# Earlier inputs, other PSUM banks and half products: three edits around the first steady unit of a fused recurrence and maxout FFN

## The chip, the cores and the metric

The kernel runs on one NeuronCore of a Trainium2 chip. The metric is the device time of one execution in microseconds; the number for a kernel is the median over its runs. Everything is FP32 on the device.

## The reference

A gated linear recurrence (an attention block) is computed for 4 batches x 8 heads over 768 tokens with head size 48; its output, with the heads side by side, is the input of a maxout FFN.

```python
# q, k, v, f_logit: (4, 8, 768, 48)
f = 1.0 / (1.0 + np.exp(-f_logit))
for t in range(S):
    state = f[:, :, t, :, None] * state + np.einsum('bhd,bhe->bhde', k[:, :, t], v[:, :, t])
    y[:, :, t] = np.einsum('bhd,bhde->bhe', q[:, :, t], state)
x = y.transpose(0, 2, 1, 3).reshape(3072, 384)
h = np.maximum(np.maximum(x @ w1, x @ w2), x @ w3)      # w1, w2, w3: (384, 768)
return h @ w_out                                        # w_out: (768, 384)
```

## The kernel before

The sequence is cut into chunks of 64 tokens. A **unit** is one chunk of two batches, 128 token rows, with all 8 heads; there are 24 units (`NU`). Four units make a **group** of 512 tokens (`TOK`), and the FFN is run by groups, six of them.

For one unit u these helpers emit the work:

- `load` and `load_v` issue DMAs on the sync queue (SP). For u below 8 (`BY_ROWS`), f, k and q come as one DMA each with token rows on the partitions, v as two DMAs. f, k and q have four slots by u mod 4, and v has four tiles (`NLD`), so unit 4 writes where unit 0 was read.
- `sigmoids` turns f into gates: for u below 8, TensorE transposes the rows into PSUM (`transposed`, L278) and ScalarE applies the sigmoid (L295).
- `scan`, `after`, `before`: VectorE's running products of the gates (L316, L334), and k and q multiplied by them (kh at L327, qh at L338). k and q reach these through `features`, which for u below 8 are TensorE transposes as well.
- `keys` (L354), `pairs` (L379, masked by VectorE at L382), `values` (L394 or L398), `sums` (L419, added to the state by VectorE at L427) and `finish` (L465) or, for the first four units, `y_by_tokens` (L438, L443) and `x_of_tokens` (L454) compute the unit's output and carry the state. `pack` moves a finished group into the layout of the FFN by DMA.

PSUM has several small pools with their own banks: `ps_tr` (two tiles named "tr") for transposes, `ps_f` (two tiles named "p") for FFN products, `ps_a` and `ps_y` with one tile each. For units 0 to 3, k and q are turned in the "p" banks, for units 4 to 7 in "tr"; f always in "tr".

`ffn` is a generator. For each of six column blocks j of the hidden layer it emits three **products**, one for each of w1, w2, w3: three matmuls of 128 x 512 accumulate into one "p" bank (L513), and then ScalarE copies the first product out (L518) or VectorE takes the maximum (L520). For group 0 the first two blocks are done in two halves of 256 tokens, which makes 12 small products ahead of 12 of full width. Then come four **output products**, each six matmuls of 128 x 384 (L538), a copy and two DMAs. `fill(n)` resumes the generator until it has yielded n times. A small product has one yield, a full or an output product has two, both behind it; so `fill(2)` is one full product, and of two `fill(1)` in a row one does a product and the other nothing.

The weights arrive as 64-bit words in 24 **pieces** (18 of w1 to w3, 6 of w_out), 12 of them in raw buffers at a time, and are rounded to FP32 on the device: ScalarE (L228, L229, L232), VectorE (L239, L240, or L242 from the tenth piece on) and GpSimd (L246). Nine pieces are issued before the first unit's work; the others by `load_weights(2, done)` (L208), called in `ffn` after each product of group 0, which also emits the next rounding.

The order on every engine is the order of the code (`manual_schedule`): a prologue written out by hand for units 0 to 3 and the loads of unit 4, then a loop over units 4 to 23. The prologue's end and the loop's fills are:

```python
                y_by_tokens(3)
                load(GRP, one, "q")
...
                fill(2)
                before(GRP)
                carry(GRP)
                fill(2)
                for u in range(GRP, NU):
                    n = u + 1
                    fill(0 if u == 2 * GRP else 4 if u % 2 and u > 2 * GRP else 2)
...
                    fill(1 if u < 2 * GRP else 2)
```

Of the kernel before, what the change touches and what calls it, by code (L numbers as in the profile page):

```python
# [55 lines left out]
def kernel(  # L56
# [20 lines left out]
    NJ = DFF // 128  # L77
    GRP = 4
    TOK = GRP * UT
# [9 lines left out]
    def fast():  # L89
        ctx = ExitStack()  # L90
        with ctx:
# [74 lines left out]
            def load(u, queues=one, names="fkq"):  # L166
                for nm, src in (("f", f_logit), ("k", k), ("q", q)):
                    if nm not in names:
                        continue
                    if u < BY_ROWS:  # L170

                        c, bp = divmod(u, 2)
                        queues[NAMES.index(nm) % 2].dma_start(  # L173
                            out=rows[nm][u % 4][:, :, 0:D],
                            in_=src[2 * bp:2 * bp + 2, :, c * C:(c + 1) * C, :].rearrange("b h t d -> t b h d"))
                    elif u % 2 == 0:
                        t0 = u // 2 * C
                        for n in range(C // 32):
                            for par in range(2):
                                for e0, w in ((0, 32), (32, D - 32)):  # L180
                                    p0 = par * DP + e0
                                    nc.sync.dma_start(
                                        out=blocks[nm][u // 2 % 2][p0:p0 + 32, n, :, 0:w],
                                        in_=src[:, par::2, t0 + n * 32:t0 + (n + 1) * 32, e0:e0 + w].rearrange(
                                            "b h t d -> t (b h) d"))

            def load_v(u, queues=one):
                load_tokens(v_tiles[u % NLD], v, u, queues)
# [85 lines left out]
            def transposed(nm, u, name="tr"):  # L274

                t = {"tr": ps_tr, "p": ps_f}[name].tile([128, HP, 2, C], FP32, name=name)
                for hp in range(HP):
                    nc.tensor.transpose(t[:, hp].rearrange("p a t -> p t a"), slots[nm][u % 4][:, hp * 128:(hp + 1) * 128],  # L278
                                        ident)
                return t.rearrange("p h a t -> p a h t")  # L280
# [20 lines left out]
            def features(nm, u):  # L301

                if u < BY_ROWS:
                    return transposed(nm, u, "p" if u < GRP else "tr")
                t = work.tile([128, 2 * HP, C], FP32, name=f"{nm}t", bufs=1)
                turned(t, block(nm, u))
                return by_batch(t)
# [3 lines left out]
            def scan(u):  # L311
                gate = gate_tiles[u % 2]
                if u >= BY_ROWS:
                    turned(gate[:, :, 1:], ready[u])
                r = r_tiles[u % 2]
                nc.vector.tensor_tensor_scan(r[:, 0:LEN][:, ::-1], flat(gate)[:, ::-1], flat(from_one)[:, ::-1], 1.0,  # L316
                                             op0=ALU.mult, op1=ALU.max)
                whole = r[:, 0:LEN].rearrange("p (x t) -> p x t", t=C + 1)[:, :, 1]
                nc.vector.reciprocal(from_inv[u % 2][:, :, 0], whole)
# [85 lines left out]
            def sums(u):  # L405

                d, v_ld = ready[u], v_tiles[u % NLD]
                y = d["y"]
                if u < NU - 2:


                    apart = u < GRP
                    if apart:
                        y = ps_a.tile([128, 2, 512], FP32, name="a")
                    Y = HP * C
                    for hp in range(HP):
                        for par, a in FOUR:
                            s = slice(a * C, (a + 1) * C)
                            nc.tensor.matmul(y[par * DP:(par + 1) * DP, a, Y + hp * D:Y + (hp + 1) * D],  # L419
                                             lhsT=d["ks"][s, 2 * hp + par, :], rhs=v_ld[s, 2 * hp + par, 0:D],  # L420
                                             start=apart and hp == 0, stop=(hp == HP - 1), skip_group_check=True)
                    ds = y[:, :, Y:Y + HP * D]
                    new = states[u % 2].rearrange("p (a h) d -> p a (h d)", a=2)
                    if u < 2:
                        nc.scalar.copy(new, ds)  # L425
                    else:
                        nc.vector.tensor_tensor(new, ds, d["state"].rearrange("p (a h) d -> p a (h d)", a=2), op=ALU.add)  # L427
# [66 lines left out]
            def ffn(g, xT):  # L494
                hm = work.tile([128, NJ, TOK], FP32, name="hm", bufs=1)


                steps = [(j, slice(0, TOK)) for j in range(NJ)]
                if g == 0:
                    steps = [(j, slice(n * HALF, (n + 1) * HALF)) for n in range(2) for j in range(J_HALF)] + steps[J_HALF:]  # L500
                done, n_step = 1, 0
                for j, t in steps:
                    w = t.stop - t.start
                    for i in range(3):
                        p = ps_f.tile([128, TOK], FP32, name="p")[:, 0:w]
                        for kt in range(NK):
                            if g:
                                rhs = xT[:, kt, :]
                            elif w < TOK:
                                rhs = by_halves(xT)[:, t.start // HALF, kt, :]  # L510
                            else:
                                rhs = by_halves(xT)[:, :, kt, :]
                            nc.tensor.matmul(p if g or w < TOK else p.rearrange("p (two t) -> p two t", two=2),  # L513
                                             lhsT=w_in[i][:, kt, j * 128:(j + 1) * 128], rhs=rhs,
                                             start=(kt == 0), stop=(kt == NK - 1))
                        if i == 0:
                            top = work.tile([128, TOK], FP32, name="top")[:, 0:w]
                            nc.scalar.copy(top, p)  # L518
                        else:
                            nc.vector.tensor_tensor(hm[:, j, t] if i == 2 else top, p, top, op=ALU.max)  # L520

                        if g == 0:
                            n_step += 1
                            ahead = n_step + 1 if n_step <= 6 else 7 + (n_step - 6) * 5 // 6 if n_step <= 12 else 12 + (n_step - 12) * 6 // 5
                            for r in range(done, min(ahead, len(pieces))):
                                if r + 2 < len(pieces):
                                    round_begin(r + 2)
                                if r + 1 < len(pieces):
                                    round_end(r + 1)
                                done = r + 1  # L530
                            load_weights(2, done)
                        yield
                        if w == TOK:
                            yield
                for i in range(GRP):
                    p = ps_f.tile([128, TOK], FP32, name="p")
                    for j in range(NJ):
                        nc.tensor.matmul(p[:, 0:DM], lhsT=hm[:, j, i * UT:(i + 1) * UT], rhs=w_out[:, j, :],  # L538
                                         start=(j == 0), stop=(j == NJ - 1))
                    o = work.tile([UT, DM], FP32, name="o", bufs=3)  # L540
                    nc.scalar.copy(o, p[:, 0:DM])  # L541
                    c, bp = divmod(g * GRP + i, 2)
                    for a in range(2):
                        t0 = (2 * bp + a) * S + c * C
                        last = g * GRP + i == NU - 1 and a
                        (nc.scalar if last else nc.sync).dma_start(out=out[t0:t0 + C, :], in_=o[a * C:(a + 1) * C, :])
                    yield
                    yield

            pending = []  # L550
# [24 lines left out]
            with tc.manual_schedule():  # L575
# [25 lines left out]
                y_by_tokens(0)  # L601
                keys(1)
                sums(0)
                scan(2)
                after(2)
                pairs(1)
# [23 lines left out]
                fill(1)  # L630
                keys(3)
                sums(2)
                load(GRP, one, "fk")
                y_by_tokens(2)
                pairs(3)
                fill(1)
# [4 lines left out]
                sums(3)  # L641
                fill(1)
                y_by_tokens(3)
                load(GRP, one, "q")
                load_v(GRP)
                load(GRP + 1)
                load_v(GRP + 1)
                x_of_tokens(3, xT)
# [324 lines left out]
```

## Time and profile before

| | us |
|---|---|
| median of 10 runs | 480.62 (478.46 to 482.48) |
| the profiled execution | 479.17 |
| its span (first to last instruction) | 477.4 |
| TensorE busy in the span | 457.6 (96%) |
| VectorE, ScalarE, GpSimd busy | 267.0, 145.8, 104.3 |
| mean granted TensorE clock | 0.994 |

A row of a timeline or a group tells the engine, the line, the tiles written and read, the shape and the count. TensorE shows two records for each FP32 matmul. "SPq" is the sync engine's queue issuing a DMA: its duration is the time of the issue, not of the transfer. A wait is put down to what released it last. A chain of waits follows the end of the program back to its beginning.

### The profile page before, as it was taken

What the parts mean: (1) busy time and instruction counts of PE and PEld (TensorE: products, weight loads), DVE (VectorE), ACT (ScalarE), POOL (GpSimd) and SP (SyncE); (2) the same over time, 40 slices, a digit from 0 to 9 for tenths busy, and PEclk for the clock granted to TensorE, in tenths of its full rate; (3) what the DMA queues carried; (4) which work ended last, traced back from release to release, by engine and by line L of the source; (5) the groups of instructions that cost most, each with busy time, mean ns of one, the idle gap of its engine ahead of it and who ended that gap; (6) DMA issues with size and microseconds to landing.
All of it is one profiled execution on the core that took longest, in us unless ns stands there. A gap on an engine that the chain in (4) does not pass through costs nothing.

```text
span 477.4 us, 10233 instructions
## 1 busy us (share of the span) xinstructions
PE 457.6 (96%) x4068; PEld 250.4 (52%) x4068; DVE 267.0 (56%) x528; ACT 145.8 (31%) x339; POOL 104.3 (22%) x125
## 2 busy tenths in 40 slices
PE   4989699999999999999999999999999999999995
PEld 3877555555555445554455554455554445544453
DVE  6876476767487584577684587694575220021110
ACT  2444367522012133243243243243343211100000
POOL 2153444432330230320330321330311300000000
PEclk9999899999999999999999999999999999999999
DMA  9999996215477444576634487534470012100002
GB/s 134 217 286 266 211 206 82 45 35 94 84 97 113 115 82 104 96 144 88 153 68 109 92 150 89 160 69 106 95 146 4 0 51 50 35 1 1 2 17 52
DMA packets 177141, 47.13 MB, mean 99 GB/s; under 512 B 154816, under 2 KB 175552, under 8 KB 177088
## 3 DMA queue, kind: packets, MB, share of 16 engines
q1 hardware_dynamic: 172528, 45.25, 48.4%
q10 hardware_dynamic: 4560, 1.18, 1.5%
q8 instruction: 33, 0.54, 0.5%
q14 instruction: 20, 0.16, 0.1%
HBM read 37.75 MB, written 4.72 MB: 89 GB/s over the span
## 4 chain that ended last, share of the span: by engine, by line
PE 88%; SPq 3%; DMA 3%; DVE 3%; ACTq 1%; issue 1%; ACT 0%; DVEq 0%
PE p L513 59%; PE p L538 18%; PE y L465 3%; PE y L398 2%; SPq L173 2%; PE a L379 2%; PE y L419 2%; DMA q_ld<-in_q_dram 2%; DMA raw<-in_moe_w_dram 1%; PE tr L278 1%; SPq L163 1%; ACTq L486 1%; DVE r L316 1%; DVE prod L334 0%; PE tr L354 0%
## 5 line engine op out<-in xcount | busy, mean ns | idle before, releaser
L513 PE MATMUL p<-xT,w_in 128*128 128x512 f32 (+1 forms) x684 | 291.1, 577 | 0.4 <-POOL w_in L246 0.4
L513 PEld LDWEIGHTS p<-xT,w_in 128*128 128x128 f32 x684 | 127.5, 191 | 133.2 <-issue 125.6
L538 PE MATMUL p<-w_out,hm 128*128 128x384 f32 x288 | 96.3, 489 | 0.0
L520 DVE TENSOR_TENSOR top<-p,top 128x512 f32<-128x512 f32 (+1 forms) x38 | 24.9, 656 | 104.8 <-PE p L513 104.8
L538 PEld LDWEIGHTS p<-w_out,hm 128*128 128x128 f32 x288 | 54.0, 190 | 37.6 <-issue 1.9
L369 DVE STREAM_TRANSPOSE ks<-kh 32x128 f32<-32x128 f32 x224 | 67.7, 302 | 3.6
L518 ACT COPY top<-p 128x512 f32<-128x512 f32 (+1 forms) x38 | 21.4, 562 | 150.6 <-PE p L513 150.6
L326 POOL COPY ends<-r 128x8 f32<-128x8 f32 x24 | 6.7, 277 | 188.0 <-DVE r L316 188.0
L520 DVE TENSOR_TENSOR hm<-p,top 128x512 f32<-128x512 f32 (+1 forms) x38 | 24.8, 652 | 34.4 <-PE p L513 34.4
L327 POOL TENSOR_TENSOR kh<-kt,r 128x512 f32<-128x512 f32 x16 | 31.4, 1961 | 36.5 <-DVE kt L283 23.9
L541 ACT COPY o<-p 128x384 f32<-128x384 f32 x24 | 11.4, 476 | 86.7 <-PE p L538 83.3
L316 DVE TENSOR_TENSOR_SCAN r<-gate,from_one 128x520 f32<-128x520 f32 x24 | 29.8, 1240 | 10.9 <-ACT gate L295 7.0
L471 ACT COPY heads<-y 64x256 f32<-64x256 f32 (+1 forms) x60 | 22.2, 369 | 44.9 <-PE y L465 38.5
L334 DVE TENSOR_TENSOR_SCAN prod<-gate,from_inv 128x520 f32<-128x520 f32 x24 | 30.8, 1285 | 0.0
L246 POOL TENSOR_TENSOR w_in<-top_bits,rest_bits 128x384 uint32<-128x384 uint32 x18 | 20.3, 1133 | 35.6 <-DVE top_bits L242 15.8
L382 DVE TENSOR_TENSOR at<-a,mask 128x512 f32<-128x512 f32 x24 | 16.5, 689 | 12.0 <-PE a L379 11.6
L283 DVE STREAM_TRANSPOSE gate<-sig 128x512 f32<-128x512 f32 x16 | 11.3, 705 | 15.5 <-ACT sig L298 15.5
L344 POOL TENSOR_TENSOR state<-st,ends 128x384 f32<-128x384 f32 x22 | 19.2, 873 | 0.7 <-ACT st L425 0.6
L338 POOL TENSOR_TENSOR qh<-qt,prod 128x512 f32<-128x512 f32 x16 | 18.9, 1179 | 0.6 <-DVE qt L283 0.5
L398 PEld LDWEIGHTS y<-at,v_ld 64*64 64x64 f32 x640 | 11.1, 134 | 14.1 <-issue 9.0
L465 PEld LDWEIGHTS y<-qh,state 48*48 48x48 f32 x640 | 10.3, 119 | 12.7 <-issue 11.6
L379 PE MATMUL a<-qh,kh 48*64 48x64 f32 x768 | 16.2, 223 | 0.2
(89 smaller groups left out, 311.9 us busy)
## 6 DMA issues: line engine op xcount, KB each, us to landing
raw<-in_moe_w_dram SPq DMA_DIRECT2D x36, 384.0 KB, 6.0
v_ld<-in_v_dram SPq DMA_DIRECT2D x48, 96.0 KB, 3.6
raw<-in_moe_w_out_dram SPq DMA_DIRECT2D x12, 384.0 KB, 4.5
out_dram<-o SPq DMA_DIRECT2D x47, 96.0 KB, 2.2
xT<-heads SPq DMA_DIRECT2D x30, 72.0 KB, 2.2
f_ld<-in_f_logit_dram SPq DMA_DIRECT2D x32, 64.0 KB, 2.6
k_ld<-in_k_dram SPq DMA_DIRECT2D x32, 64.0 KB, 2.6
q_ld<-in_q_dram SPq DMA_DIRECT2D x32, 64.0 KB, 3.1
```

The lines of the kernel that those rows point to most:

```text
L316: nc.vector.tensor_tensor_scan(r[:, 0:LEN][:, ::-1], flat(gate)[:, ::-1], flat(from_one)[:, ::-1], 1.0, op0=ALU.mult, op1=ALU.max)
L327: (nc.vector if u < BY_ROWS else nc.gpsimd).tensor_tensor(kh.rearrange("p h a t -> p a h t"), kt, by_batch(r[:, 1:LEN + 1].rearrange("p (x ...
L334: nc.vector.tensor_tensor_scan(flat(prod), flat(gate_tiles[u % 2]), flat(from_inv[u % 2]), 1.0, op0=ALU.mult, op1=ALU.max)
L369: nc.vector.transpose(ks[n * 32:(n + 1) * 32, :, par, e0:e0 + 32], kh[p0:p0 + 32, :, a, t0:t0 + 32])
L379: nc.tensor.matmul(p[t, par, hp * C:(hp + 1) * C], lhsT=kh[r, hp, a, :], rhs=qh[r, a, hp, :], start=True, stop=True)
L398: nc.tensor.matmul(y[o:o + DP, a, hp * C:(hp + 1) * C], lhsT=v_ld[s, 2 * hp + par, :], rhs=d["at"][s, par, hp, :], start=(hp == 0), stop=F ...
L465: nc.tensor.matmul(y[o:o + D, a, hp * C:(hp + 1) * C], lhsT=st[r, a, hp, :], rhs=d["qh"][r, a, hp, :], start=False, stop=(hp == HP - 1), s ...
L471: nc.scalar.copy(heads[o, :, t0 + a * C:t0 + (a + 1) * C], y[i, a, 0:HP * C].rearrange("p (h t) -> p h t", h=HP))
L513: nc.tensor.matmul(p if g or w < TOK else p.rearrange("p (two t) -> p two t", two=2), lhsT=w_in[i][:, kt, j * 128:(j + 1) * 128], rhs=rhs, ...
L518: nc.scalar.copy(top, p)
L520: nc.vector.tensor_tensor(hm[:, j, t] if i == 2 else top, p, top, op=ALU.max)
L538: nc.tensor.matmul(p[:, 0:DM], lhsT=hm[:, j, i * UT:(i + 1) * UT], rhs=w_out[:, j, :], start=(j == 0), stop=(j == NJ - 1))
```

## The change

Three edits. The loads of unit 4 (f, k, q and v) are issued after `sums(0)` in the code; on the sync queue this is right behind the nine early weight pieces and ahead of the tenth. `features` turns k and q of unit 3 in the "tr" banks in place of the "p" banks. In `ffn` a full product yields after its second matmul of three and at its end, and an output product after its third matmul of six and at its end, where both yields stood at the end before. The number of yields is the same.

```diff
@@ features
-                    return transposed(nm, u, "p" if u < GRP else "tr")
+                    return transposed(nm, u, "p" if u < GRP - 1 else "tr")
@@ ffn
                             nc.tensor.matmul(p if g or w < TOK else p.rearrange("p (two t) -> p two t", two=2),
                                              lhsT=w_in[i][:, kt, j * 128:(j + 1) * 128], rhs=rhs,
                                              start=(kt == 0), stop=(kt == NK - 1))
+                            if kt == 1 and w == TOK:
+                                yield
...
                         yield
-                        if w == TOK:
-                            yield
                 for i in range(GRP):
                     p = ps_f.tile([128, TOK], FP32, name="p")
                     for j in range(NJ):
                         nc.tensor.matmul(p[:, 0:DM], lhsT=hm[:, j, i * UT:(i + 1) * UT], rhs=w_out[:, j, :],
                                          start=(j == 0), stop=(j == NJ - 1))
+                        if j == NJ // 2 - 1:
+                            yield
...
-                    yield
                     yield
@@ prologue
                 keys(1)
                 sums(0)
+                load(GRP)
+                load_v(GRP)
                 scan(2)
...
                 sums(2)
-                load(GRP, one, "fk")
                 y_by_tokens(2)
...
                 y_by_tokens(3)
-                load(GRP, one, "q")
-                load_v(GRP)
                 load(GRP + 1)
                 load_v(GRP + 1)
```

## The prediction

> **What bounds the kernel now.** I read the page first (engine totals, the 40 slices), then TensorE's waits, then timelines and windows around the longest of them.
>
> ```profile
> PE 457.6 (96%) x4068; PEld 250.4 (52%) x4068; DVE 267.0 (56%) x528; ACT 145.8 (31%) x339; POOL 104.3 (22%) x125
> ...
> PE   4989699999999999999999999999999999999995
> ...
> PEclk9999899999999999999999999999999999999999
> DMA  9999996215477444576634487534470012100002
> ```
>
> TensorE is busy everywhere but in slices 1, 3 and 5 (slice 5 is 47.7 to 59.7 us, and the clock dips there too). After about 60 us a gain can only come from work that TensorE no longer waits for. The DMA engines are full in the first six slices, so there each load's place in the order counts. TensorE's waits:
>
> ```profile
> PE tr L278 <- DMA q_ld<-in_q_dram: 4.2, 1, 4.2
> ...
> PE p L438 <- DVE st L427: 0.9, 1, 0.9
> PE y L465 <- DVE st L427: 0.8, 1, 0.8
> ...
> PE p L278 <- ACT top L518: 0.5, 1, 0.5
> ```
>
> The first, third and fourth stand where the diff works. The timeline of TensorE around the first (start, duration, instruction), and two windows (window, length, busy time and count of PE, PEld, DVE, ACT, POOL; then clock, DMA share, GB/s):
>
> ```profile
> 44.76 2.76 PE L513 MATMUL p<-xT,w_in 128*128 128x256 f32 x12
> 51.72 0.90 PE L278 MATMUL tr<-ident,q_ld 128*128 128x128 f32 x4 [4.20 <-DMA q_ld<-in_q_dram]
> 52.41 6.80 PE L513 MATMUL p<-xT,w_in 128*128 128x256 f32 x24
> ```
>
> ```profile
> 48.00:51.70 3.70, 0.00 (x0) 0.02 (x1) 2.02 (x4) 1.47 (x4) 2.58 (x2) 1.00 1.23 198
> 51.70:55.40 3.70, 3.69 (x12) 3.06 (x13) 0.88 (x2) 0.00 (x0) 0.00 (x0) 0.54 1.10 152
> ```
>
> A product of the first group at half width is 6 records. TensorE ends products 7 and 8, stands until q of unit 4 lands, and then runs at clock 0.54 for 3.7 us. The sync queue shows why q is late: it is issued at 42.99, behind six weight pieces, and takes 8.6 us to land.
>
> ```profile
> 23.61 8.52 SPq L208 DMA_DIRECT2D raw<-in_moe_w_dram  x10
> 32.22 0.95 SPq L173 DMA_DIRECT2D f_ld<-in_f_logit_dram  x1
> 33.26 3.95 SPq L173 DMA_DIRECT2D k_ld<-in_k_dram  x1
> 37.31 4.96 SPq L208 DMA_DIRECT2D raw<-in_moe_w_dram  x5
> 42.38 0.52 SPq L208 DMA_DIRECT2D raw<-in_moe_w_out_dram  x1
> 42.99 0.68 SPq L173 DMA_DIRECT2D q_ld<-in_q_dram  x1
> ```
>
> **Part 1, the loads of unit 4.** Five issues move: f and k from 32.2 and 33.3, q from 43.0, the two of v from 43.8 and 46.5, all to about 27.8, right after the ninth piece (the tenth is issued there now). What they overwrite was last read by unit 0, whose last reader, the sums at L419 (TensorE, start 22.55), is done by 23.2; so I add no wait on the sync queue. Nothing of this goes through POOL's or ACT's queue.
> How long do they take in the DMA engines? By landing times, q of unit 5 is down 1.5 us after its k (56.7 and 55.2), k and q of unit 6 are 1.2 and 1.3 us after the load before: 1.3 us for each of f, k, q, and about as much for the two halves of v, 5.2 us in all. The window 50 to 56 us says the same: 4708 packets in 6.0 us, nearly all under 512 B, and the four loads are 4 x 1024 packets of 192 B.
> A rule speaks against the move. The Trainium skill, "DMA: Bandwidth & Descriptors", Specifications, asks for at least 512 B per transfer for line rate; putting small packets in front of the 1 KB packets of the weights then costs dearly. If each 192 B packet cost as much as 512 B at the 341 GB/s which that page's table gives for 1 MB, 4096 of them take 6.1 us (an estimate from the page). I take the trace's 5.2; the sum below is the same with either, because what pays is the next item.
> Who is later: piece 10 lands at 27.84 + 8.9 = 36.8 now, and at about 42.0 then (42.9 by the rule). Its first user is the ACT rounding at L228, start 46.52; cover 4.5 us. Pieces 11 to 14 follow at some 1.1 us each (42 to 47), against roundings at 48.0 and then, after product 10, from about 50.9. So they cost nothing. Were that cover gone, ACT is in order: behind the rounding stand the copy of product 10's bank, the keys of unit 4 and the sigmoid of unit 5, and TensorE would stand microsecond for microsecond. From f of unit 5 on, the same bytes lie ahead as before, so those loads land when they do now.
> What goes: the 4.20 us wait, since q lands near 40. And the slow clock: q's transposes and 24 records took 52.41 - 51.72 + 59.04 - 52.41 = 7.32 us; at full clock a record of this kind starts every 0.216 us (12 in 2.59) and the four transposes take 0.44, so 5.6; 1.7 us goes with the wait.
> What comes instead: vector work that ran in the shadow of the wait. DVE does the scan of before(4) (48.82, 1.23 us), then qh at L338 (0.69), and only then empties product 9's bank (L520, 0.42): 51.2 us. TensorE, with two banks, reaches product 11 at 47.5 + 0.44 + 2.59 = 50.5. New wait +0.7, between 0 (if the scheduler's wait is looser than I read) and 1.0.
> What is late next: f of unit 5. Its landing is not in the trace; between the second half of v (46.52 + 6.7 = 53.2) and k of unit 5 (49.88 + 5.3 = 55.2) I put it at 54.2. Its transposes start at 60.20 now and at 60.20 - 4.20 - 1.7 + 0.7 = 55.0 then: 0.8 us of cover, the thinnest of all. k and q of unit 5 have about 3 us (63.27 and 63.71 less 5.2, against 55.2 and 56.7), f of unit 6 nearly 5 (74.74 - 5.2 against 59.35 + 5.3). Part 1: -4.2 - 1.7 + 0.7 = -5.2 us.
>
> **Part 2, k and q of unit 3 in the transpose banks.** Same 8 transposes. The 0.5 us wait of q's transposes on ACT L518 at 27.5 should go, for the transpose banks' last readers there (24.17 + 0.46 at the latest) are done. But TensorE waits again at 32.72 for DVE L427, and DVE's rows from 22.58 to 32.68 are back to back: qh (30.18) waits for DVE's own scan of 1.86 us. The time moves from one wait to the other: 0 us, bounds -0.1 and +0.3 (later users of these banks, keys of unit 3 at 30.64 and x at 35.33, find kh and qh finished at 26.9 and 30.9). If DVE were not the chain here, it would be worth 0.5.
>
> **Part 3, halves.** No instruction is added; only odd fills differ, in units 4 to 7. In units 4 and 6 the last fill leaves the third matmul of a product to the next unit, and with it the bank's emptying and the rounding emitted there (one piece on ACT, DVE and POOL); all weight issues are past by then, so SP is untouched. In unit 7 the last fill, empty now, gets the second half of an output product, 6 records of 0.32 us = 1.94 us, between the sums at L419 (end 109.0) and finish(7) at L465; its copy and two output DMAs follow it, behind the loads of unit 10 on SP, and nothing waits for them.
>
> ```profile
> 108.39 0.63 PE L419 MATMUL y<-v_ld,ks 64*64 64x48 f32 x32
> 109.80 0.66 PE L465 MATMUL y<-qh,state 48*48 48x64 f32 x32 [0.78 <-DVE st L427]
> ```
>
> The wait lasts until DVE's 0.56 us are over (109.19 + 0.56), so 1.94 covers it: -0.8 us, from then on to the end, as TensorE has only one wait of 0.3 us later. Against it: held-open banks could stall a product; at most one copy, 0.4 us, in units 5 and 7. I take -0.8, bounds -0.8 and 0.
>
> **Sum.** -5.2 + 0 - 0.8 = -6.0 us. The profiled execution took 479.17 (span 477.4 and 1.77 around it); it becomes 473.2. It lies 1.45 below the median of the ten runs, 480.62, which becomes **474.6**.
>
> **Rivals.**
> A, f of unit 5 becomes the wait. For it: 0.8 us of cover at an estimated landing, and the sync queue stalls for 2 to 4 us in single rows. Against: DMA is full around it, so order alone moves nothing. Two us late leaves -4.0: 476.6. Here the clock matters again. The trace has one gap long enough to show a loss, 4.2 us for 1.7, pro rata 0.8 for 2 us. The skill ("TensorE: Matmul & The Clock Gate", Part 1: The HAM clock gate) says only an idle window of about 3.4 us, free-running, halves the clock; then 2 us costs none. The 0.9 us wait at 32.72 ran on at clock 1.00, so I follow the rule; by the row it is 477.4.
> B, slower: the sync queue blocks at the moved issues. Its rows for such loads show up to 2.04 us for f, 3.95 for k, 2.40 for q, and 2.67 and 1.22 for the halves of v: 12.3 us if all five fall out so at 27.8, in place of 5.2, with everything behind 7.1 later. f of unit 5 lands at 61.3, 6.3 after TensorE asks; with the clock's 1.7 the sum is -6.0 + 8.0 = +2.0: 482.6. It decides from a landing after about 59.3. Against it: those stalls end as earlier loads land (k's at 37.2, when piece 10 is down at 36.8), so they are the engines' own backlog, already in 5.2.
> C, the move is no move: q's issue is held for something late (a bank or tile read that I missed) and only part 3 acts: -0.8, 479.8, no change that can be told.
>
> **How the numbers follow.** Forecast 0.70 (473.0 to 475.8 with the bounds of the terms), A 0.19 (475.8 to 479), B 0.07, C 0.04. Under 0.3%, 1.44 us, a measurement of this kernel cannot tell from no change: faster is the forecast and A, 0.89; same C, 0.04; slower B, 0.07. The range reaches into A to 477.8, leaving out its end, B and C; its low end, 473.0, is the sum without the new wait and with part 2's 0.1, and 0.8 for the runs' scatter.
>
> **What would show it.** Right: no TensorE idle time between 47 and 52 us, clock 1.00 throughout 24 to 470, product 11 behind a DVE wait under 1 us, first full-width product at about 55.5 instead of 60.69, no wait at L465 near 104, f, k, q of unit 4 issued from 27.8 at little over 1 us each, span near 471.4. Wrong: TensorE waiting for f_ld near 55 (A), ACT idle before L228 for raw, or SP rows of several us at 28 to 36 with DMA share falling (B), q_ld still issued after 40 (C).

## The result and the profile after

| | before | after |
|---|---|---|
| median of all runs, us | 479.87 (51 runs) | 475.66 (14 runs) |
| ratio to before, 95% interval | | 0.9915 [0.9897, 0.9933] |
| the profiled execution, its span | 479.17, 477.4 | 474.65, 472.9 |

The change takes 0.85%, about 4.1 us, where 6.0 were forecast. (The granted clock is on record for 16 executions of the changed kernel: these 14 and two profiled ones.) The page of the changed kernel (engine totals, TensorE's 40 slices, its clock):

```profile
PE 456.7 (97%) x4068; PEld 249.4 (53%) x4068; DVE 267.2 (57%) x528; ACT 145.8 (31%) x339; POOL 105.2 (22%) x125
...
PE   4989999999999999999999999999999999999995
...
PEclk9989999999999999999999999999999999999999
```

The idle slice 5 is full now. But the dip of the clock did not go: it moved from slice 5 to slice 3. TensorE's waits in the changed kernel:

```profile
PE p L438 <- DVE st L427: 1.5, 1, 1.5
...
PE p L513 <- DVE hm L522: 0.7, 1, 0.7
PE p L538 <- DVE top L522: 0.6, 1, 0.6
```

(L522 is L520 of before, shifted by the diff.) The wait for q of unit 4, that on ACT L518 and that at L465 are gone. The wait before L438 has grown from 0.9 to 1.5 us, and the two others are new. The timeline of TensorE at these places:

```profile
31.77 0.19 PE L438 MATMUL p<-st 128*1 128x1 f32 x2 [1.52 <-DVE st L427]
...
33.35 2.81 PE L513 MATMUL p<-xT,w_in 128*128 128x256 f32 x6
...
48.01 0.60 PE L278 MATMUL tr<-ident,q_ld 128*128 128x128 f32 x4
...
51.90 2.86 PE L513 MATMUL p<-xT,w_in 128*128 128x256 f32 x12 [0.69 <-DVE hm L522]
...
100.26 2.20 PE L538 MATMUL p<-w_out,hm 128*128 128x384 f32 x6 [0.63 <-DVE top L522]
```

Product 3, six records at 33.35, takes 2.81 us; products of this size took 1.56 before. Windows of the changed kernel (the clock is the third number from the end):

```profile
26.00:32.50 6.50, 4.98 (x121) 4.24 (x123) 5.45 (x9) 1.97 (x4) 4.88 (x5) 1.00 1.01 327
32.50:36.00 3.50, 3.50 (x45) 2.81 (x37) 0.69 (x1) 0.93 (x2) 0.00 (x0) 0.51 0.76 171
```

With the starts of products 1, 7 and 13 (the first of full width) and the end of finish(7) as marks, the two profiled executions differ so:

| stretch | before, us | after, us | difference |
|---|---|---|---|
| start to product 1 | 25.54 | 24.61 | -0.93 |
| product 1 to 7 (banks) | 19.22 | 20.81 | +1.59 |
| product 7 to 13 (loads) | 15.93 | 10.82 | -5.11 |
| product 13 to finish(7) (halves) | 49.78 | 50.03 | +0.25 |
| from there to the end | 366.97 | 366.67 | -0.30 |

Of the edits only k's four transposes of unit 3 lie in the first row, whose end is set by the rounding of the first weight piece on GpSimd (L246), so its -0.93 is put down to scatter: in the profiles of this document product 1 starts between 24.57 and 25.79. So theory T: the loads bring what was forecast, the bank edit costs half-clock time, the halves give back what they save. The rival is the prediction's own sum (banks 0, halves -0.8), with the loads bringing less.

### The profile page after: what moved, and what is told of

It is laid out like the page before. It is cut to its first block, busy times and chain, and to the rows that moved or that the text cites. A ratio compares the mean times of both kernels' runs of the same rounds, so it can differ in the third digit from the quotient of the medians.

```text
span 472.9 us, 10233 instructions
## 1 busy us (share of the span) xinstructions
PE 456.7 (97%) x4068; PEld 249.4 (53%) x4068; DVE 267.2 (57%) x528; ACT 145.8 (31%) x339; POOL 105.2 (22%) x125
## 4 chain that ended last, share of the span: by engine, by line
PE 88%; SPq 5%; DVE 2%; DMA 1%; ACT 1%; issue 1%; ACTq 1%; DVEq 0%
PE p L513 59%; PE p L538 18%; PE y L465 3%; PE y L398 3%; SPq L173 2%; PE a L379 2%; PE y L419 2%; SPq L163 2%; SPq L208 1%; PE tr L278 1%; DMA raw<-in_moe_w_dram 1%; ACTq L486 1%; DMA xT<-heads 0%; PE tr L354 0%; ACT heads L471 0%
## 5 line engine op out<-in xcount | busy, mean ns | idle before, releaser
L538 PE MATMUL p<-w_out,hm 128*128 128x384 f32 x288 | 96.6, 490 | 0.6 <-DVE top L522 0.6
L522 DVE TENSOR_TENSOR top<-p,top 128x512 f32<-128x512 f32 (+1 forms) x38 | 24.9, 656 | 102.1 <-PE p L513 101.6
L538 PEld LDWEIGHTS p<-w_out,hm 128*128 128x128 f32 x288 | 53.8, 190 | 38.4 <-issue 1.7
L520 ACT COPY top<-p 128x512 f32<-128x512 f32 (+1 forms) x38 | 21.3, 561 | 139.7 <-PE p L513 139.5
L522 DVE TENSOR_TENSOR hm<-p,top 128x512 f32<-128x512 f32 (+1 forms) x38 | 24.8, 652 | 34.1 <-PE p L513 34.1
L246 POOL TENSOR_TENSOR w_in<-top_bits,rest_bits 128x384 uint32<-128x384 uint32 x18 | 20.9, 1170 | 31.6 <-DVE top_bits L240 13.8
L465 PEld LDWEIGHTS y<-qh,state 48*48 48x48 f32 x640 | 10.3, 119 | 12.3 <-issue 12.3
```

Source lines behind the costliest of these rows:

```text
L465: nc.tensor.matmul(y[o:o + D, a, hp * C:(hp + 1) * C], lhsT=st[r, a, hp, :], rhs=d["qh"][r, a, hp, :], start=False, stop=(hp == HP - 1), s ...
```

## The experiments

**The loads alone** (e1_loads).

```diff
                 sums(0)
+                load(GRP)
+                load_v(GRP)
...
-                load(GRP, one, "fk")
...
-                load(GRP, one, "q")
-                load_v(GRP)
```

> The kernel before with the loads of unit 4 moved, nothing else. The step of the prediction: -5.2 us, with a new wait of about 0.7 us at product 11. Theory T (the changed kernel's trace, where everything from product 7 to the first full-width product takes 10.82 us in place of 15.93): -5.1 us in one execution, and, since the two idle stretches near 27 and 32 us stay apart, no half-clock window there: the mean clock is 0.998 or more in most executions. Then this kernel alone is about as fast as the whole change or up to 1 us faster: 474 to 476. Rival (the loads bring only what the whole change brought, because the weights behind them come late): -4.2 or less, and a wait for raw or f_ld on TensorE or ACT near 55 us.

473.60 us, 0.9864 [0.9836, 0.9891]: one third of the diff alone brings more than the whole. From product 7 to 13 it took 10.94 us, from 1 to 7 19.22. Its windows, to be held against those above:

```profile
26.00:32.50 6.50, 5.17 (x83) 4.00 (x83) 6.22 (x10) 2.07 (x4) 4.71 (x5) 1.00 0.96 284
32.50:36.00 3.50, 3.50 (x78) 3.14 (x79) 1.38 (x3) 1.32 (x3) 0.59 (x1) 1.00 1.03 241
```

TensorE stands nearly as long before 32.5 us (1.33 us against 1.52), but in pieces of 0.46 and 0.87; and the clock stays full. All six executions had a mean clock of 0.998 or more. The rival falls: the loads bring the whole of what they were to bring.

**The banks alone** (e2_banks).

```diff
-                    return transposed(nm, u, "p" if u < GRP else "tr")
+                    return transposed(nm, u, "p" if u < GRP - 1 else "tr")
```

> The kernel before with only k and q of unit 3 in the transpose banks. The step of the prediction: 0 us, the 0.5 us wait at 27.5 us moves to the wait for DVE L427. Theory T: the same move, but the joined idle stretch of about 1.4 us before L438 fills enough of one activity window that the clock is halved for 3.4 us right after it in about half of the executions: 0 to +1.7 us in one execution, +0.8 in the mean, mean clock lower than before. Rival (the bank's wait did cost time): -0.5 us.

479.46 us, 0.9993 [0.9975, 1.0011]: no change in time, though the trace shows the loss. TensorE's timeline and a window of this kernel:

```profile
32.70 0.19 PE L438 MATMUL p<-st 128*1 128x1 f32 x2 [1.52 <-DVE st L427]
...
51.40 0.63 PE L278 MATMUL tr<-ident,q_ld 128*128 128x128 f32 x4 [2.31 <-DMA q_ld<-in_q_dram]
```

```profile
33.20:36.60 3.40, 3.40 (x59) 2.92 (x51) 0.69 (x1) 0.93 (x2) 0.03 (x1) 0.50 1.10 358
```

Products 1 to 7 took 20.79 us, as in the whole change. But TensorE then came later to the wait for q, and stood 2.3 us there, against 4.2 in the profile of before: q lands when the DMA queue lets it, and up to that moment lost time is free: the transposes of q start at 51.40 here and at 51.72 in the profile of before. This shorter wait was not followed by a half clock either. So the +0.8 that I had expected of the bank edit is wrong for this kernel; it can only show once q is early.

**The halves alone** (e3_halves).

```diff
+                            if kt == 1 and w == TOK:
+                                yield
...
                         yield
-                        if w == TOK:
-                            yield
...
+                        if j == NJ // 2 - 1:
+                            yield
...
-                    yield
                     yield
```

> The kernel before with only the half products. The step of the prediction: -0.8 us, the wait at L465 near 110 us gone. Theory T: that wait is gone, but the output product waits some 0.6 us for a bank that VectorE empties late (L520, first maximum of the last block), and each extra change between FFN and attention matmuls costs TensorE some 0.1 to 0.15 us more; -0.1 to +0.3 us, not to be told from none in the median, but to be read in the trace from the start of the first full-width product to the end of finish(7): 49.6 us before, 49.5 to 49.9 here.

480.15 us, 1.001 [0.9987, 1.0033]. From product 13 to the end of finish(7) 50.04 us, 0.26 more than before, with the wait at L465 gone and a new one ahead of the output product:

```profile
106.01 2.20 PE L538 MATMUL p<-w_out,hm 128*128 128x384 f32 x6 [0.64 <-DVE top L522]
...
111.36 0.67 PE L465 MATMUL y<-qh,state 48*48 48x64 f32 x32
```

This kernel still waits for q: 5.6 us in its profile, and its clock was halved for two windows there.

**Loads and halves, no banks** (e4_loads_halves): the first and third edits together.

> The whole change without its bank edit (k and q of unit 3 stay in the p banks). The step of the prediction: the same time as the whole change, 475.7. Theory T: 0.8 us faster in the mean, since no half-clock window follows the wait before L438; mean clock 0.998 or more in most executions, against eight of sixteen executions of the whole change. Against the loads alone: equal within 0.3 us.

475.70 us, 0.9893 [0.9865, 0.9922]. The clock was as expected: 0.998 or more in all six executions, and products 1 to 7 took 19.23 us. The time was not: 475.70 is the whole change's 475.66, and 2 us above the loads alone. Part of that is another wait that its profile shows, on VectorE and then on TensorE:

```profile
282.36 0.71 DVE L283 STREAM_TRANSPOSE qt<-q_ld 128x512 f32<-128x512 f32 x1 [2.63 <-DMA f_ld<-in_f_logit_dram]
```

```profile
283.70 1.12 PE L513 MATMUL p<-xT,w_in 128*128 128x512 f32 x2 [1.76 <-DVE top L522]
```

VectorE stands for q of unit 14 (the instruction reads q; the row names the load of f, whose issues follow q's on the queue), and behind it in order is the maximum that frees TensorE's bank. Three of the ten profiles up to e8_q_beside_k (this one, e2_banks and e6_loads_banks) have TensorE standing there, for about 2 us each; the others, with and without the edits, have at most 0.6 us of it, on VectorE alone. The last run below takes it up.

**Output products alone by halves** (e5_loads_outhalf): the loads, and of the halves only the yield after `j == NJ // 2 - 1`.

> The loads moved, and only the output products given out by halves (full products whole). Theory H (in the runs with halves, the stretch from the first full-width product to the end of finish(7) takes 50.04 us against 49.78 without, though the 0.78 us wait at L465 is gone: 0.64 goes to a new wait for VectorE's L520 before the output product, and 0.4 to extra changes between FFN and attention matmuls): splitting the full products is what makes the last block's maximum late, so here neither that wait nor most of the extra changes is there, and the stretch takes about 49.2; 0.6 us less than the loads alone, 473.0. Rival (the half output product itself brings the wait): 49.8 to 50.1, as with all halves.

473.48 us, 0.9884 [0.9859, 0.9908]; from product 13 to finish(7) 49.13 us, 0.65 less than with full products and outputs both whole. TensorE's timeline has no wait in it:

```profile
98.47 2.10 PE L538 MATMUL p<-w_out,hm 128*128 128x384 f32 x6
...
101.57 2.20 PE L538 MATMUL p<-w_out,hm 128*128 128x384 f32 x6
103.71 0.66 PE L465 MATMUL y<-qh,state 48*48 48x64 f32 x32
```

So the half output product does cover the wait at L465; the split of the full products is what brings the wait at L538. VectorE's timeline of the whole change shows how: the maximum of the last block's second product now stands behind the gates and the scan of unit 8.

```profile
98.17 1.24 DVE L316 TENSOR_TENSOR_SCAN r<-gate,from_one 128x520 f32<-128x520 f32 x1
99.45 0.21 DVE L319 RECIPROCAL from_inv<-r 128x8 f32<-128x8 f32 x1
99.57 0.64 DVE L522 TENSOR_TENSOR top<-p,top 128x512 f32<-128x512 f32 x1
```

Here 0.38 us of TensorE's gain was spent on a wait for f of unit 5; the median does not tell this kernel from the loads alone.

**Loads and banks** (e6_loads_banks): the first and second edits.

> The loads moved and k and q of unit 3 in the transpose banks, no halves. Theory C (the joined idle stretch before L438 lets the clock be halved for 3.4 us): from the first product to the seventh 19.2 us in executions without, 20.8 in those with it; mean clock 0.997 or less in about half of the executions where the loads alone had 0.998 or more in all six; median 0 to 1.6 us over the loads alone, 473.6 to 475.2. Rival (the bank edit is free, and the whole change's lower clocks came from elsewhere): clock as with the loads alone, 473.6.

475.40 us, 0.9912 [0.9885, 0.9939]; products 1 to 7 20.83 us. Windows:

```profile
26.00:34.10 8.10, 6.58 (x150) 5.64 (x149) 6.59 (x11) 2.74 (x6) 5.31 (x5) 1.00 0.98 306
34.10:37.50 3.40, 3.40 (x19) 2.70 (x10) 1.07 (x3) 0.64 (x2) 0.00 (x0) 0.50 1.00 152
```

The mean clock was 0.996 or less in four of seven executions. Over all kernels with the loads (in e8_q_beside_k only q) moved, that is 11 of 23 executions with the bank edit and its gap (7 of 16 of the whole change, 4 of 7 here) and none of 48 without it. The rival falls. The profiled execution, 479.71, is far the slowest of the seven: it also stood 2.04 us for the maximum behind q of unit 14, and its clock was halved a second time after that.

**Product 9 first** (e7_loads_order): the loads, and

```diff
-                fill(2)
+                fill(3)
                 before(GRP)
                 carry(GRP)
-                fill(2)
+                fill(1)
```

> The loads moved, and product 9 put ahead of before(4) in the order, so that VectorE empties its bank before the scan and qh of unit 4. Theory: the 0.70 us wait at product 11, which took the place of the wait for q, goes; the keys and pairs of unit 4 still find kh and qh ready; from product 7 to the first full-width product 10.2 us in place of 10.9; -0.7 us against the loads alone, 472.9. Rival (another wait stands behind it, for the rounding ScalarE and VectorE do there or for f of unit 5): 10.9 and 473.6.

473.74 us, 0.9895 [0.9866, 0.9924]. The wait at product 11 is gone, from product 7 to 13 it took 10.39 us in place of 10.94; of the 0.7 us, 0.5 went to the next wait in line, f of unit 5. In the median nothing shows (expected 472.9).

**Only q moved** (e8_q_beside_k).

```diff
-                load(GRP, one, "fk")
+                load(GRP)
...
-                load(GRP, one, "q")
```

> The kernel before with only q of unit 4 moved: issued right behind f and k of unit 4, behind the thirteenth weight piece, not behind the ninth; v stays. Theory Q (what pays is only that q no longer stands behind six weight pieces): q lands near 43, before TensorE asks at 47.5, and from product 7 to the first full-width product it takes 10.9 us as with all loads moved; 473.6 to 474. Rival W (the place behind the ninth piece matters, since behind the thirteenth the sync queue stalls and q comes after 47.5): a wait at q of 1 to 3 us remains, 475 to 478.

474.23 us, 0.9901 [0.9875, 0.9926]; from product 7 to 13 10.82 us, no wait for q. The sync queue:

```profile
37.78 2.68 SPq L173 DMA_DIRECT2D q_ld<-in_q_dram  x1
40.56 3.10 SPq L208 DMA_DIRECT2D raw<-in_moe_w_dram  x5
```

q landed 5.5 us after its issue, at about 43.3, and TensorE asked for it at 46.6. It is enough that q does not stand behind six weight pieces; in this stretch the other loads ahead of the tenth piece bring nothing more, and the medians (474.23, and 473.60 with all loads moved) do not tell the two apart. Rival W falls.

**Output halves and product 9 first** (e9_loads_outhalf_order): e5 and e7 together.

> The loads moved, output products by halves, product 9 ahead of before(4). Theory F (behind the waits that went stands f of unit 5, for which TensorE stood 0.4 and 0.5 us in the two kernels before with one of these edits): the wait at product 11 and the one at L465 are both gone, and TensorE stands about 0.5 us for f of unit 5; 0.9 us less than the loads alone, 472.7. Rival (both gains add up with no wait behind them): 1.3 us less, 472.3.

472.07 us, 0.9838 [0.9803, 0.9873]. Both waits are gone, and TensorE stands 0.9 us for f of unit 5, almost twice what I expected. By the wait theory F holds; the median lies nearer to the rival's 472.3, and does not decide between them:

```profile
54.21 0.63 PE L278 MATMUL tr<-ident,f_ld 128*128 128x128 f32 x4 [0.90 <-DMA f_ld<-in_f_logit_dram]
```

**The whole change, idle stretch filled** (e10_after_busy). The three added matmuls feed nothing.

```diff
+                busy(3)
                 y_by_tokens(2)
```

> The whole change with three extra matmuls of 128 x 256 on TensorE, whose results nobody reads, in the idle stretch before L438. Theory C (half-clock window after the joined idle stretch): the stretch is filled by 1.3 us of work that costs nothing, no half-clock window near 33 us, from the first product to the seventh 19.2 us, mean clock 0.998 or more in nearly all executions; median 0.8 us below the whole change's 475.7. Rival (the lost 1.6 us is something else in the order of the transpose banks): 20.8 us from the first product to the seventh, and 475.7.

473.83 us, 0.9875 [0.9841, 0.9909]; products 1 to 7 19.10 us. Timeline and windows:

```profile
30.36 1.56 PE L565 MATMUL p<-from_one,ident 128*128 128x256 f32 x6
31.86 0.19 PE L438 MATMUL p<-st 128*1 128x1 f32 x2
```

```profile
26.00:32.50 6.50, 6.50 (x123) 5.30 (x123) 5.63 (x9) 1.97 (x4) 5.06 (x5) 1.00 1.00 313
32.50:36.00 3.50, 3.50 (x59) 2.98 (x51) 1.99 (x5) 1.42 (x3) 0.00 (x0) 1.00 1.06 203
```

The same order of banks at a full clock costs nothing; useless work brings the 1.6 us back (20.81 to 19.10). The clock was 0.997 or more in all six executions. The median fell by 1.8 us, more than the 0.8 expected.

**Two more loads earlier** (e11_f_and_q_earlier): e9, and

```diff
                 x_of_tokens(2, xT)
+                load(GRP + 1, one, "f")
...
-                load(GRP + 1)
+                load(GRP + 1, one, "kq")
...
+                    if BY_ROWS <= u + 2 < NU and u % GRP == 0:
+                        load(u + 2, one, "q")
                     if CHECKS <= u + 2 < CHECKS + len(pieces) // 2:
                         check_load(2 * (u + 2 - CHECKS))
                         check_load(2 * (u + 2 - CHECKS) + 1)
-                    if BY_ROWS <= u + 2 < NU and u % GRP == 0:
-                        load(u + 2, one, "q")
```

> As the loads with output halves and product 9 first, and two more loads put earlier: f of unit 5 ahead of the last four weight pieces issued before it, and in the loop q of units 10, 14, 18 and 22 ahead of the check's two weight pieces. Theory F: no wait for f of unit 5 near 55 us, and no wait of about 2 us near 284 us for q of unit 14, which three of the ten profiles show; 472.2 with less scatter between executions. Rival (the earlier f pushes the last weight pieces or k and q of unit 5 into the next wait): 472.7 to 474.

471.31 us, 0.9822 [0.9789, 0.9855], six executions within 0.9 us: faster than before, and than the whole change, whose interval lies above. Neither wait is in the profile, and products 7 to 13 take 9.86 us.

```profile
53.29 0.66 PE L278 MATMUL tr<-ident,f_ld 128*128 128x128 f32 x4
53.78 1.45 PE L513 MATMUL p<-xT,w_in 128*128 128x512 f32 x3
```

**The loads, and q of unit 14 earlier** (e12_loads_q14): the loads, and the last part of that diff.

> The loads moved, and in the loop q of units 10, 14, 18 and 22 ahead of the check's two weight pieces. Theory: q of unit 14 lands about 2 us earlier against VectorE's need of it near 279 us, so that no execution stands there; the median is that of the loads alone or 0.3 us lower, 473.3 to 473.6, and executions above 475 are gone. Rival (the wait near 284 us comes from a late transfer that its place in the queue does not change): as the loads alone, with the same high executions.

472.83 us, 0.9854 [0.9822, 0.9887]. Six executions lie between 472.67 and 473.13, where the loads alone had 472.89 to 474.89. VectorE finds q there:

```profile
277.24 1.20 DVE L334 TENSOR_TENSOR_SCAN prod<-gate,from_inv 128x520 f32<-128x520 f32 x1
278.36 0.68 DVE L283 STREAM_TRANSPOSE qt<-q_ld 128x512 f32<-128x512 f32 x1
```

One profile without the wait proves little, since seven of the ten had none. The spread says more: 0.5 us here and 0.9 in e11_f_and_q_earlier, the two kernels with q of unit 14 earlier, against 1.5 to 3.3 in the other kernels that have the loads moved and no bank edit. That speaks for the cause; six executions each do not settle it.

## Why the prediction was right, and where it was not

**Loads: right.** Forecast -5.2, measured -5.11 from product 7 to 13, and -4.99 with the loads alone. The terms fit too: the new wait at product 11 was 0.69 (forecast 0.7), and the order on VectorE is its cause (e7 removes it). The tenth piece landed at about 42 (forecast 42.0), before ScalarE's first need at 47.18. The next in line was f of unit 5, as said: it landed at about 54.3 (forecast 54.2), asked for at 55.74. Rival A became real only where more was taken away (e5, e7, e9).
What was wrong in it is a detail: I expected the moved loads to be issued at little over 1 us each. k took 4.90 us and q 2.53 at the sync queue, as rival B had it:

```profile
28.44 4.90 SPq L173 DMA_DIRECT2D k_ld<-in_k_dram  x1
33.43 2.53 SPq L173 DMA_DIRECT2D q_ld<-in_q_dram  x1
```

The other sign of B came with q's row: from 33.5 to 35.9 the DMA engines were busy only 0.66 of the time. So the reason given against B, that such stalls are the engines' own backlog, fits k's row (DMA share 1.00 from 29.0 to 32.5 us) and not q's; why the queue stood there is open. B's consequence did not come: q landed at 39.9 and f of unit 5 when forecast, so nothing that TensorE needed was late.
How much the loads bring differs between executions, since the wait that they remove does: it was 4.2, 2.3 and 5.6 us in the three profiles with q at its old place. In the medians they brought 6.2 us (479.83 to 473.60), 1.0 more than the term.

**Banks: the step that failed**, though its working held. The time did move from the wait on the bank to the wait before L438, as written (0.9 to 1.5 us), and VectorE's chain did not move by more than about 0.1 us, counted from product 1. I took it for 0 with bounds of -0.1 and +0.3, and looked at the length of the idle time alone. Put together, 1.5 us in a row were followed by 3.4 us at half clock, +1.59 us in the profiled execution. The Trainium skill ("TensorE: Matmul & The Clock Gate", Part 1: The HAM clock gate), which I followed in rival A, names an idle window of about 3.4 us. The measurement differs, and decides: 1.5 us in a row had it, and 0.46 and 0.87 apart never did in 48 executions. Not in every execution either: 11 of 23. Nor is the length of the gap the whole rule; the last section shows what the traces tell of that. The step also missed that edit 1 removes the cover of edit 2: ahead of the wait for q, lost time was free.
The size in the medians is less sure than the cause. The bank edit costs 1.8 us in two comparisons (e6_loads_banks against e1_loads, the whole change against e10_after_busy), more than half of 1.6, and nothing in a third (the whole change against e4_loads_halves, which has the wait for q of unit 14 in its profile).

**Halves: the term was mis-sized.** -0.8 was the wait at L465, and that went (-0.78). The bound "held-open banks could stall a product; at most 0.4 us" was there but too small and not taken: the late bank at L538 costs 0.64. The other 0.4 us of the +0.26 I put to extra changes between the FFN's matmuls and the others: with the output product in two parts of 2.13 us in place of one of 3.96, 0.3 us is read from the starts in the trace; the rest is not shown.

**Sum.** -5.1 + 1.6 + 0.25 and the two rows outside the edits (-0.93, -0.30) make the 4.5 us between the profiled executions. The forecast's sign, its main term and its range were right; two of its three edits do not help. That the median came within 1.1 us of the forecast is partly luck: in the medians the loads brought 1.0 more than their term, and the other two edits, which were to bring 0.8, gave 2.1 back (473.60 to 475.66). One sum was off without effect: with the bounds of the terms the upper end of the forecast is 476.0 (474.6 + 0.3 + 0.3 + 0.8), not 475.8.

## What to carry to other kernels

Price idle time by where it lies, not only by how much there is: joining two short waits of the busiest engine into one can cost more than both. When two edits act one behind the other, ask of each what the other's wait was hiding: an edit that measures as free can be so because a later wait absorbs it. And when a unit of work is cut so that its result comes later, follow who empties it: a queue in order behind it has other work, and half of this edit, the half whose wait was seen, was worth having.

## What the runs showed of the hardware that I had not expected

The clock was halved for one window of 3.4 us after TensorE had been idle for only 1.5 us in a row (busy 4.98 of the 6.5 us before it, in the changed kernel), in about half of the executions. With 5.17 of 6.5 us busy, in two gaps, it stayed full in every execution of the loads alone, and with the gap filled it did too. The section of the Trainium skill cited above says that the window runs freely. The traces agree: within each of them the clock changes at times that lie whole multiples of 3.413 us apart (20.48, 37.55 and 457.39 us are 6, 11 and 134 of them), on a grid that lies differently in each execution. In all three profiles with the gap unfilled, the 1.5 us lie wholly in the one stretch of this grid before the half clock (29.08 to 32.50 in the changed kernel). As an estimate, a gap of 1.52 us falls wholly into a stretch of 3.41 in 55% of its positions, (3.41 - 1.52) / 3.41; 11 of 23 is 48%. No profile was kept of an execution in which the gap was there and the clock stayed full.

The wait near 284 us tells more. In e6_loads_banks TensorE stood 2.04 us, all in one stretch; in e2_banks 2.08 us, of which 0.84 fell before a border of the grid and 1.24 behind it; in e4_loads_halves 1.76 us, all in one stretch. The windows, cut at each trace's borders, in this order:

```profile
283.28:286.69 3.41, 1.37 (x4) 0.57 (x4) 2.39 (x5) 0.00 (x0) 1.60 (x2) 1.00 0.57 70
286.69:290.10 3.41, 3.41 (x6) 1.35 (x5) 2.27 (x8) 0.00 (x0) 0.37 (x1) 0.50 0.73 92
```

```profile
285.80:289.21 3.41, 2.17 (x5) 1.06 (x6) 3.35 (x9) 0.00 (x0) 1.97 (x2) 1.00 0.72 87
289.21:292.60 3.39, 3.39 (x22) 1.36 (x24) 1.24 (x5) 0.59 (x1) 0.00 (x0) 1.00 0.71 87
```

```profile
281.16:284.58 3.42, 1.66 (x4) 0.49 (x3) 2.22 (x4) 0.00 (x0) 1.43 (x2) 1.00 0.50 61
284.58:287.99 3.41, 3.41 (x9) 1.52 (x8) 2.44 (x9) 0.59 (x1) 0.54 (x1) 1.00 0.75 93
```

Only the first was followed by a half clock. The first two waits differ little but in how the border cuts them; this pair fits the grid, and one pair is no proof. Nor is it idle time alone that decides: 1.76 us idle in one stretch left the clock full here, and 1.52 before L438 did not. Around the wait of 1.76 us stand products of 128x512, before L438 many small matmuls; whether that is the difference, no run here shows.

The issue of a DMA on the sync queue took up to 4.9 us (k of unit 4 in the changed kernel), and no wait of TensorE came of it: q, issued behind it, landed at 39.9 us and was needed at 48.0.
